# Per-column scale vectors spread over the partitions by TensorE instead of VectorE's stream shuffle

## The chip, the cores and the metric

The kernel runs on one core of a Trainium2 chip. The time is the device time of that core in microseconds (us), the median of several runs. A core has TensorE (PE; matmuls, whose results go to the accumulator memory PSUM), VectorE (DVE), ScalarE (ACT), GpSimd (POOL), SyncE (SP), and DMA engines that move data between HBM and the on-chip memory SBUF. SBUF has 128 partitions. GpSimd, SyncE and ScalarE issue the transfers, each in the order of its own program.

## The reference

Attention with 16 query heads and 4 key heads on 8 batches, and then a residual block with a token mix and a channel mix. All inputs are f32.

```python
x = attention(q, k, v)                     # per batch: 384 tokens x 1024 columns
a1 = alpha1 * x + beta1                    # alpha1, beta1, alpha2, beta2, lam: 1024 columns each
tok = w_tok @ a1                           # 384 x 384 over the tokens
u = x + lam * tok
a2 = alpha2 * u + beta2
ch = relu(a2 @ w_ch1) @ w_ch2              # 1024 -> 4096 -> 1024
out = u + lam * ch
```

The five vectors have one number per column. Where VectorE multiplies a tile that has tokens on the partitions, it needs each vector in every one of the 128 partitions: a `vecs` tile of 128 x 4 x 1024 f32 with g1 = alpha1 * lam, h1 = beta1 * lam, al2 = alpha2 and lam. How that tile is filled is what the change is about.

## The kernel before

W2 stays in SBUF (loaded once, in 16 pieces). W1 is loaded anew for each batch in 16 chunks of 512 KB (in SBUF, bf16), into a ring of 5. The loads turn f32 into bf16 and are issued by GpSimd. Batch 0's attention and token mix are a lead-in; then for each batch a pass over W1 (line 400, `h`) and one over W2 (line 438, `ch`) follow, and the attention of the next batch is woven into the W2 part. In the lead-in, `at[i]` lists what stands after the i-th group of scores in the program. Each `yield` of a pass is a numbered place, at which `turns` hangs work.

```python
vecs = const.tile([P, 4, DM], f32, tag="vecs", name="vecs")
g1, h1, al2, lam_t = (vecs[:, i] for i in range(4))
...
def load_w1(n):                                    # chunk n into the ring, issued by GpSimd
    t = sb.tile([P, NDT, CW * P], bf, tag="w1", name="w1", bufs=RING)
    nc.gpsimd.dma_start(out=t, in_=w1src[:, :, c * CW * P:(c + 1) * CW * P])
...
nc.vector.memset(vecs[:, 0:4:3, :512], 0.0)
def load_vec(i, ap, lo, n):                        # the vector into partitions 0, 32, 64, 96
    nc.sync.dma_start(out=vecs[0:P:32, i, lo:lo + n],
                      in_=bass.AP(tensor=ap.tensor, offset=ap.offset + lo, ap=[[0, 4], [1, n]]))
load_vec(0, moe_alpha1, 0, 512)
load_vec(3, moe_lam, 0, 512)
...
def spread(i, half):                               # from there into the other 31 of each 32
    t = vecs[:, i, half * 512:(half + 1) * 512]
    nc.vector.stream_shuffle(out=t, in_=t, mask=[0] * 32)
def scale(i, half, eng=nc.gpsimd):                 # times lam
    t, m = (vecs[:, j, half * 512:(half + 1) * 512] for j in (i, 3))
    eng.tensor_tensor(out=t, in0=t, in1=m, op=MUL)
...
load_q4(3)                                         # GpSimd's program from here
place_k(0, 0, (0,))
units = side(0)
for f in units[:8]: f()                            # lead-in, first units
scale(0, 0)
load_w1(0)
load_w1(1)
place_k(0, 1)
split()                                            # beta1 * lam as three bf16 rows, for the bias
nc.gpsimd.memset(stage[:, 2120:2824], 0.0)
nc.gpsimd.memset(vecs[:, 0:4:3, 512:], 0.0)
load_vec(0, moe_alpha1, 512, 512)
load_vec(3, moe_lam, 512, 512)
load_w1(2)
load_w1(3)
nc.gpsimd.memset(vecs[:, 1:3], 0.0)
load_w1(4)
load_k(1)
load_vec(1, moe_beta1, 0, DM)
load_vec(2, moe_alpha2, 0, DM)
load_q(1)
load_v(1)
for i in range(3): load_w2(0, i, 8)
for f in units[8:]: f()
...
# in main(0), after chunk c of W1:
if b or c + RING < NCH:
    load_w1(b * NCH + c + RING)                    # into the ring place that chunk c has left
# loading of the third batch's q, in main(1):
if b == 1 and c in range(1, 5):
    load_q(2, [G * (c - 1)])
```

The last lines, and the turning of the third batch's q by TensorE, are in both kernels.

Of the kernel before, what the change touches and what calls it, by code (L numbers as in the profile page):

```python
# [12 lines left out]
def kernel(  # L13
# [21 lines left out]
    nc = tc.nc  # L35
    f32 = mybir.dt.float32
    bf = mybir.dt.bfloat16
    EXP = mybir.ActivationFunctionType.Exp
    RELU = mybir.ActivationFunctionType.Relu
    MUL = mybir.AluOpType.mult  # L40
    ADD = mybir.AluOpType.add
    SUB = mybir.AluOpType.subtract
# [4 lines left out]
    DM = Hq * D  # L47
    DFF = moe_w_ch1.shape[1]
    P = 128
# [4 lines left out]
    NP = Hq // 2  # L54
# [3 lines left out]
    RING = 5  # L58
# [13 lines left out]
    ident = const.tile([P, P], bf, tag="ident", name="ident")  # L72
# [3 lines left out]
    vecs = const.tile([P, 4, DM], f32, tag="vecs", name="vecs")  # L76
# [54 lines left out]
    def load_w1(n):  # L131
        if n < B * NCH:
            t = sb.tile([P, NDT, CW * P], bf, tag="w1", name="w1", bufs=RING)
            c = n % NCH
            nc.gpsimd.dma_start(out=t, in_=w1src[:, :, c * CW * P:(c + 1) * CW * P])  # L135
            w1_tiles[n] = t
# [5 lines left out]
    def bank(shape, tag, name, dtype=f32):  # L142
        if tag == "three":
            return threes[0].tile(shape, dtype, tag="sc", name=name, bufs=3)
        if tag == "mm":
            return mms.tile(shape, dtype, tag="mm", name=name, bufs=2)
        return psum.tile(shape, dtype, tag=tag, name=name, bufs=2 if tag == "sc" else 1)
# [9 lines left out]
    def evac(eng):  # L157
        return nc.scalar.copy if eng == "ACT" else nc.vector.tensor_copy
# [16 lines left out]
    def side(b):  # L175
# [136 lines left out]
        def rows_r(tag):  # L312
            ps = bank([P, 512], tag, "r")
            for st in range(NST):
                nc.tensor.matmul(out=ps[:32, :S], lhsT=ones, rhs=wtokT[:, st, :], start=(st == 0),
                                 stop=(st == NST - 1))
            turned = ps[:, S:S + 2 * NP].rearrange("p (i n) -> p i n", i=2)
            for i, c in enumerate((2, 3)):
                nc.tensor.matmul(out=turned[:, i], lhsT=rows_f[:NP, c * P:(c + 1) * P], rhs=ident_f[:NP, :NP],
                                 is_transpose=True, start=True, stop=True, skip_group_check=True)  # L320
            t = hTf[:32, 7296:7296 + S]
            nc.scalar.copy(out=t, in_=ps[:32, :S])
            nc.vector.scalar_tensor_tensor(out=R[:32], in0=t, scalar=masks[2], in1=ps[:32, :S], op0=MUL, op1=ADD)
            nc.vector.tensor_copy(out=al2T, in_=turned[:, 0])
            nc.vector.tensor_copy(out=a2T[:, :, S:S + 1], in_=turned[:, 1, :, None])

        us = []

        def add(f, *a):
            us.append(lambda: f(*a))  # L330
# [11 lines left out]
        if not first:  # L342


            turns = {24 + 8 * i: [(q_transpose, 2 * i, 2, "three")] for i in range(4)} if b == 2 else {}
            if b == 1:
                turns = {4: [(spread, 1, 0)], 6: [(spread, 1, 1)], 8: [(scale, 1, 0), (scale, 1, 1), (spread, 2, 0)],
                         10: [(spread, 2, 1)], 12: [(k_transpose, 0)], 16: [(q_transpose, 0, 2, "av")],
                         20: [(k_transpose, 2)]}
                for i in range(3):  # L350
                    turns[24 + 4 * i] = [(q_transpose, 2 + 2 * i, 2, "av")]
            return turns, {
                0: [(scores3, 0)], 4: [(av, 0)], 6: [(scores3, 1)], 8: [(tok_flip, 0)], 11: [(av, 1)],
                13: [(scores3, 2, True)], 15: [(av, 2)], 16: [(tok_flip, 1)], 18: [(tok_flip, 2)], 19: [(av, 3)],
                21: [(scores3, 3)], 23: [(tok_flip, 3)], 25: [(av, 4)], 27: [(scores3, 4)], 29: [(tok_flip, 4)],
                31: [(av, 5)], 33: [(scores3, 5, True)], 35: [(av, 6), (tok_flip, 5)], 37: [(av, 7)],
                39: [(tok_flip, 6)], 41: [(tok_flip, 7)]}
        add(k_transpose, 0, 1)
        add(q_transpose, 0, 1, "av", "ACT")
        add(place_k, 0, 0, (1,))  # L360
        add(q_transpose, 1, 1, "tp")
        ut = a2_transpose
        at = {0: [(warmup, 3), (spread, 0, 0), (spread, 3, 0)], 1: [(k_transpose, 1, 1)],
              2: [(q_transpose, 2, 2, "av")], 3: [(warmup, 1)],
              4: [(av, 0)], 5: [(a1, 0)], 6: [(av, 1), (k_transpose, 2, 2, "tp")],
              7: [(q_transpose, 4, 2, "av"), (a1, 1)], 8: [(av, 2)],
              9: [(wtok_transpose, 0, "av"), (wtok_transpose, 1, "tp")],
              10: [(wtok_transpose, 2, "av"), (q_transpose, 6, 2, "mm"), (fill_h, 0)], 11: [(av, 3), (rows_r, "tp")],
              12: [(a1, 2)], 13: [(tok, 0), (av, 4), (a1, 3)],
              14: [(tok, 1), (spread, 0, 1), (spread, 3, 1), (scale, 0, 1, nc.vector), (ut, 0)], 15: [(a1, 4), (av, 5), (tok, 2), (a1, 5), (fill_h, 4)], 16: [(ut, 1), (tok, 3)],  # L370
              17: [(ut, 2), (av, 6), (a1, 6)]}
        for i in range(18):
            add(scores, i)
# [76 lines left out]
    with tc.manual_schedule(engines=order):  # L450
# [9 lines left out]
        load_k(0, [0])  # L460

        hTf = hT.rearrange("p n s -> p (n s)")
        rows_f = hTf[:32, 9216:10240].bitcast(f32)
        rows_t = hTf[:32, 10240:10496].bitcast(f32)
        rows_b = hTf[:32, 10496:10624]
        stage = sb.tile([P, NST * DM], f32, tag="x", name="stage", bufs=2)
        qst = stage[:, :G * NST * D].rearrange("p (h st d) -> p h st d", h=G, st=NST)
        wtok_in = stage[:, 1536:2112].bitcast(bf).rearrange("p (tt s) -> p tt s", tt=NST)
# [4 lines left out]
        ones = stage[:, 2824:2840].bitcast(bf)  # L473
        masks = [stage[:32, 2840 + i:2841 + i] for i in range(3)]
        sel4 = stage[:32, 2844:2848].bitcast(bf)
        nc.vector.memset(vecs[:, 0:4:3, :512], 0.0)

        def load_row(i, ap, n=4):
            nc.sync.dma_start(out=rows_f[:n * NP, i * P:(i + 1) * P],
                              in_=bass.AP(tensor=ap.tensor, offset=ap.offset, ap=[[0, n], [P, NP], [1, P]]))  # L480


        def load_vec(i, ap, lo, n):
            nc.sync.dma_start(out=vecs[0:P:32, i, lo:lo + n],
                              in_=bass.AP(tensor=ap.tensor, offset=ap.offset + lo, ap=[[0, 4], [1, n]]))

        load_vec(0, moe_alpha1, 0, 512)
        load_vec(3, moe_lam, 0, 512)
        load_k(0, [2])
        load_row(0, moe_lam)  # L490
        load_row(1, moe_beta1)
        load_row(2, moe_alpha2, 1)
        load_row(3, moe_beta2, 1)
        for h in (0, 2):
            nc.scalar.dma_start(out=qst[:, h:h + 2], in_=q[0, h:h + 2].rearrange("h (p st) d -> p h st d", st=NST))
        xs[0] = sb.tile([P, NST, DM], f32, tag="x", name="x", bufs=2)
# [10 lines left out]
        AX = mybir.AxisListType.X  # L507
# [2 lines left out]
            nc.vector.tensor_reduce(out=m, in_=ident[:32, 8 * (i + 1):24 + 8 * (i // 2)], op=ADD, axis=AX)  # L510
        nc.vector.tensor_scalar(out=masks[2], in0=masks[2], scalar1=-1.0, scalar2=None, op0=MUL)
        with nc.allow_low_precision("ones and zeros"):
            nc.vector.tensor_reduce(out=sel4, in_=ident[:32, :32].rearrange("p (k c) -> p c k", c=NP), op=ADD, axis=AX)


        def spread(i, half):
            t = vecs[:, i, half * 512:(half + 1) * 512]
            nc.vector.stream_shuffle(out=t, in_=t, mask=[0] * 32)  # L518

        def scale(i, half, eng=nc.gpsimd):  # L520
            t, m = (vecs[:, j, half * 512:(half + 1) * 512] for j in (i, 3))
            eng.tensor_tensor(out=t, in0=t, in1=m, op=MUL)


        def split():
            r = rows_f[:, P:2 * P]
            nc.gpsimd.tensor_tensor(out=r, in0=r, in1=rows_f[:, :P], op=MUL)
            for src, dst, m in ((r, rows_t, masks[0]), (rows_t, r, masks[1])):
                nc.gpsimd.tensor_copy(out=rows_b, in_=src)
                nc.gpsimd.tensor_scalar(out=dst, in0=rows_b, scalar1=m, scalar2=None, op0=MUL)  # L530
                nc.gpsimd.tensor_tensor(out=dst, in0=dst, in1=src, op=SUB)
            nc.gpsimd.tensor_copy(out=rows_b, in_=r)


        def fill_h(p):
            nc.vector.tensor_tensor(out=H[:32, p * P:(p + 4) * P].rearrange("p (n d) -> p n d", n=4),
                                    in0=rows_b[:, None, :].to_broadcast([32, 4, P]),
                                    in1=sel4[:, p:p + 4, None].to_broadcast([32, 4, P]), op=MUL)

        load_v(0)  # L540
# [1 line left out]
        nc.gpsimd.dma_start(out=wtok_in, in_=moe_w_tok.rearrange("(p tt) s -> p tt s", tt=NST))  # L542
        load_q4(3)
        place_k(0, 0, (0,))
        units = side(0)
        for f in units[:8]:
            f()
        scale(0, 0)
        load_w1(0)
        load_w1(1)  # L550
        place_k(0, 1)
        split()
        nc.gpsimd.memset(stage[:, 2120:2824], 0.0)
        nc.gpsimd.memset(vecs[:, 0:4:3, 512:], 0.0)
        load_vec(0, moe_alpha1, 512, 512)
        load_vec(3, moe_lam, 512, 512)
        load_w1(2)
        load_w1(3)
        nc.gpsimd.memset(vecs[:, 1:3], 0.0)  # L559
        load_w1(4)  # L560
        load_k(1)
        load_vec(1, moe_beta1, 0, DM)
        load_vec(2, moe_alpha2, 0, DM)
        load_q(1)
        load_v(1)
        for i in range(3):
            load_w2(0, i, 8)
        for f in units[8:]:
            f()
        place_k(1, 0)  # L570
        place_k(1, 1)
# [45 lines left out]
```

The softmax here doesn't subtract the row's maximum and nothing guards it: scores larger than these inputs give would overflow.

## Time and profile before

| what | value |
|---|---|
| median of 3 runs | 808.59 us (808.38 to 808.82) |
| span of the profiled run | 807.0 us |
| W1 matmuls, line 400 | x2016, 35% of the chain that ended last |
| W2 matmuls, line 438 | x1600, 41% of it |
| stream shuffles, line 518 | x8, median 725 ns each, between 6.9 and 44 us |
| products with lam, line 522 | x3 on GpSimd, median 1272 ns; x1 on VectorE, 692 ns |
| memsets of `vecs` on GpSimd, lines 554 and 559 | 941 and 1845 ns |

An engine's name with "q" is its queue of issued transfers, PEld is the load of a matmul's weights. In a list of waits, a line names the engine and source line that waited, what it waited for, the total, how often, and the longest. The chain of waits follows the work that ended last back to its causes: an engine in it did work that the end depended on. Idle time of an engine outside the chain costs nothing by itself. The granted TensorE clock was 1.00 in every stretch.

### The profile page before, as it was taken

Reading aid. Unit: us, or ns where it says so; the run is one execution under the profiler, and the core shown is the slowest. Engines: PE = TensorE matmul, PEld = TensorE weight load, DVE = VectorE, ACT = ScalarE, POOL = GpSimd, SP = SyncE. Lnnn points to the kernel's source line nnn. Section 1 sums busy time; section 2 is a strip of 40 time slices with the busy share of each in tenths; the row PEclk is TensorE's granted clock in tenths of the full one; section 3 lists DMA queues with packets and bytes.
Section 4 is the critical chain, followed back from the end, with each engine's and each line's share of the span. In section 5 each row is a group of like instructions: output and inputs, shape, how many; then the busy total and the mean of one; then the engine's idle time right before and its main releaser. Section 6 shows DMA issues by size and latency. Waiting matters only on the chain.

```text
span 807.0 us, 14228 instructions
## 1 busy us (share of the span) xinstructions
PE 794.0 (98%) x6123; PEld 452.2 (56%) x6123; DVE 344.9 (43%) x669; ACT 223.0 (28%) x302; POOL 189.9 (24%) x247
## 2 busy tenths in 40 slices
PE   8989999999999999999999999999999999999998
PEld 4755555555556555565555655556555655556545
DVE  7753465224652265422663236622366224652122
ACT  7522431224312324123321233222331224312100
POOL 8534220433003410135002350023400330003000
DMA  9999997999159982899529992399914995129611
GB/s 149 195 205 201 211 205 129 194 195 168 56 124 185 198 118 61 144 186 197 81 71 170 187 196 59 86 170 197 171 42 110 166 196 94 48 58 185 86 40 40
DMA packets 231767, 112.42 MB, mean 139 GB/s; under 512 B 81200, under 2 KB 225536, under 8 KB 231704
## 3 DMA queue, kind: packets, MB, share of 16 engines
q0 software_dynamic: 170752, 83.47, 78.4%
q1 hardware_dynamic: 60408, 27.65, 13.5%
q8 instruction: 48, 0.79, 0.4%
q10 hardware_dynamic: 544, 0.39, 0.2%
q14 instruction: 15, 0.12, 0.0%
HBM read 170.57 MB, written 12.58 MB: 227 GB/s over the span
## 4 chain that ended last, share of the span: by engine, by line
PE 88%; DMA 8%; POOL 2%; issue 1%; DVE 0%; POOLq 0%
PE ch L438 41%; PE h L400 35%; DMA w<-in_moe_w_ch_dram 6%; PE sc L218 4%; PE sc L253 4%; PE sc L276 3%; DMA q_raw<-in_q_dram 1%; POOL w L135 1%; PE warm L455 0%; PE tp L204 0%; POOL w L140 0%; POOL vecs L559 0%; POOL q_raw L117 0%; DVE vecs L518 0%; POOL hT L530 0%
## 5 line engine op out<-in xcount | busy, mean ns | idle before, releaser
L438 PE MATMUL ch<-w,hT 128*128 128x512 bf16 (+2 forms) x1600 | 357.6, 371 | 1.4 <-DVE o L443 0.9
L400 PE MATMUL h<-a2T,w 128*128 128x384 bf16 (+1 forms) x2016 | 331.8, 326 | 4.4 <-DMA w<-in_moe_w_ch_dram 4.2
L400 PEld LDWEIGHTS <-w 128*128 128x128 bf16 x2016 | 196.4, 98 | 135.9 <-DMA w<-in_moe_w_ch_dram 6.2
L135 POOL DMA_DIRECT2D w<-in_moe_w_ch_dram x128 | 112.3, 878 | 537.2 <-PE h L400 519.1
L438 PEld LDWEIGHTS <-hT 128*128 128x128 bf16 x1600 | 144.8, 98 | 153.1 <-issue 10.5
L227 ACT ACTIVATE es<-sc 128x1024 bf16<-128x1024 f32 x126 | 121.4, 1023 | 188.2 <-PE sc L218 179.4
L410 DVE TENSOR_SCALAR hT<-h,bias 128x384 bf16<-128x384 f32 x128 | 79.1, 618 | 215.4 <-PE h L400 214.8
L408 ACT ACTIVATE hT<-h,bias 128x384 bf16<-128x384 f32 x128 | 74.4, 581 | 306.7 <-PE h L400 306.2
L443 DVE TENSOR_TENSOR o<-ch,vecs 128x512 f32<-128x512 f32 (+2 forms) x50 | 33.5, 669 | 109.4 <-PE ch L438 109.4
L253 PEld LDWEIGHTS <-es 128*128 128x128 bf16 x1008 | 38.2, 97 | 13.2
L276 PEld LDWEIGHTS <-wtokT 128*128 128x128 bf16 x576 | 37.2, 98 | 13.6 <-DVE a L266 1.7
L218 PE MATMUL sc<-qT,kT 64*128 64x384 bf16 (+2 forms) x576 | 41.9, 272 | 0.8 <-ACT hT L227 0.7
L253 PE MATMUL sc<-v,es 128*128 128x65 bf16 x1008 | 39.8, 193 | 0.0
L258 DVE RECIPROCAL rinv<-sc 128x6 f32<-128x6 f32 x56 | 10.8, 193 | 67.2 <-PE sc L253 66.3
L283 DVE TENSOR_TENSOR x<-sc,x 128x384 f32<-128x384 f32 x56 | 30.9, 552 | 19.9 <-PE sc L276 19.9
L276 PE MATMUL sc<-a,wtokT 128*128 128x128 bf16 x504 | 37.3, 219 | 0.0
L218 PEld LDWEIGHTS <-kT 64*128 64x128 bf16 x576 | 21.7, 94 | 24.6 <-issue 19.3
L444 DVE TENSOR_TENSOR o<-o,x 128x512 f32<-128x512 f32 (+2 forms) x50 | 33.5, 670 | 1.7
L287 DVE TENSOR_TENSOR a<-x,vecs 128x384 bf16<-128x384 f32 x56 | 31.5, 562 | 1.9
L266 DVE TENSOR_TENSOR a<-a1f,vecs 128x384 bf16<-128x384 f32 x56 | 31.4, 561 | 2.1
L264 DVE TENSOR_TENSOR a1f<-x,vecs 128x384 f32<-128x384 f32 x56 | 31.2, 558 | 1.9
L259 DVE TENSOR_TENSOR x<-sc,rinv 128x384 f32<-128x384 f32 x56 | 31.2, 557 | 1.9
(78 smaller groups left out, 213.1 us busy)
## 6 DMA issues: line engine op xcount, KB each, us to landing
w<-in_moe_w_ch_dram POOLq DMA_DIRECT2D x144, 512.0 KB, 8.7
out_dram<-o SPq DMA_DIRECT2D x47, 256.0 KB, 2.2
q_raw<-in_q_dram POOLq DMA_DIRECT2D x28, 192.0 KB, 8.3
kst<-in_k_dram SPq DMA_DIRECT2D x16, 192.0 KB, 3.0
v<-in_v_dram POOLq DMA_DIRECT2D x24, 64.0 KB, 8.0
a2T<-a SPq DMA_TRANSPOSE x56, 2.3
qg<-in_q_dram POOLq DMA_DIRECT2D x3, 192.0 KB, 4.5
stage<-in_q_dram ACTq DMA_DIRECT2D x2, 192.0 KB
```

The lines of the kernel that those rows point to most:

```text
L135: nc.gpsimd.dma_start(out=t, in_=w1src[:, :, c * CW * P:(c + 1) * CW * P])
L218: nc.tensor.matmul(out=sc[:, hh, k % 4:k % 4 + n], lhsT=kT[r, sk, 2 * p // G, :], rhs=qT[r, p, st:st + n, :], start=True, stop=True)
L227: nc.scalar.activation(out=e, in_=sc, func=EXP, scale=scale_qk)
L253: nc.tensor.matmul(out=av[:, hh, sq, :], lhsT=ess[k // 4][:, m % 2, k % 4, :], rhs=vb[:, sk, hk, :], start=(sk == 0), stop=(sk == NST - 1))
L276: nc.tensor.matmul(out=ps[:, tt, :], lhsT=wtokT[:, st, tt * P:(tt + 1) * P], rhs=a1s[p][:, st, :], start=(st == 0), stop=(st == NST - 1 an ...
L287: nc.vector.tensor_tensor(out=a2s[p], in0=u, in1=bc(al2, p), op=MUL)
L400: nc.tensor.matmul(out=ps[:, :n], lhsT=w1[:, dt, j * P:(j + 1) * P], rhs=a2T[:, dt, :n], start=(dt == 0), stop=(dt == NDT - 1))
L408: nc.scalar.activation(out=hT[:, nt, :], in_=ps[:, :S], func=RELU, bias=c1)
L410: nc.vector.tensor_scalar(out=hT[:, nt, :], in0=ps[:, :S], scalar1=c1, scalar2=0.0, op0=ADD, op1=mybir.AluOpType.max)
L438: nc.tensor.matmul(out=ps[:, lo:hi], lhsT=hT[:, nt, ms * P:(ms + 1) * P], rhs=w2[:, nt, dw * 512 + lo:dw * 512 + hi], start=(nt == 0), sto ...
L443: nc.vector.tensor_tensor(out=o[:, lo:hi], in0=ps[:, lo:hi], in1=lam_t[:, c], op=MUL)
L444: nc.vector.tensor_tensor(out=o[:, lo:hi], in0=o[:, lo:hi], in1=x[:, ms, c], op=ADD)
```

## The change

The vectors are no longer shuffled. Each is loaded as rows: row p holds columns 128p to 128p + 127, so a vector is 8 partitions x 128, and most are loaded four times over into 32 partitions. Rows are scaled by lam and split by VectorE (or GpSimd) into three bf16 parts whose sum is the f32 value; the parts lie in rows p, p + 8 and p + 16. A matmul with a column of ones at these three rows, repeated 128 times as its weights (`sel`), sums the parts and writes the row into all 128 partitions of PSUM, from where it is copied to `vecs`. It is meant to take the shuffles, their memsets and the products over 128 partitions off VectorE and GpSimd. In the first pass the matmuls for h1, al2 and lam hang at places 34 to 54, with ScalarE's copies.

```diff
-        nc.vector.memset(vecs[:, 0:4:3, :512], 0.0)
-        load_vec(0, moe_alpha1, 0, 512)
-        load_vec(3, moe_lam, 0, 512)
+        sel = stage[:, 2852:2856].bitcast(bf)
+        for t in (stage[:, 2120:2824], rows_b, sel):
+            nc.vector.memset(t, 0.0)
+        load_row(0, moe_alpha1)
+        load_row(3, moe_lam)
         load_k(0, [2])
-        load_row(0, moe_lam)
         load_row(1, moe_beta1)
-        load_row(2, moe_alpha2, 1)
-        load_row(3, moe_beta2, 1)
+        load_row(2, moe_alpha2)
+        load_row(4, moe_beta2, 1)
 ...
+        def spread(ps_, vs, tag, eng="DVE"):
+            n = len(ps_)
+            ps = bank([P, 4, P], tag, "vec")
+            w = vs[1] - vs[0]
+            for i, p in enumerate(ps_):
+                nc.tensor.matmul(out=ps[:, i * w:(i + 1) * w], lhsT=sel[:, p:p + 1].to_broadcast([P, P]),
+                                 rhs=rows_b[:, vs[0] * P:vs[1] * P], start=True, stop=True)
+            evac(eng)(out=vecs[:, vs[0]:vs[1], ps_[0] * P:(ps_[-1] + 1) * P].rearrange("p v (n d) -> p n v d", n=n),
+                      in_=ps[:, :n * w].rearrange("p (n v) d -> p n v d", n=n))
 ...
-                turns = {4: [(spread, 1, 0)], 6: [(spread, 1, 1)], 8: [(scale, 1, 0), (scale, 1, 1), (spread, 2, 0)],
-                         10: [(spread, 2, 1)], 12: [(k_transpose, 0)], ...
+                turns = {4: [(split, 2, 4, 0)], 8: [(split, 2, 4, 1)], 12: [(k_transpose, 0)], ...
+                for i in range(4):
+                    turns[34 + 4 * i] = [(spread, (2 * i, 2 * i + 1), (1, 3), "tp", "ACT")]
+                for i in range(2):
+                    turns[50 + 4 * i] = [(spread, range(4 * i, 4 * i + 4), (3, 4), "av", "ACT")]
 ...
-        at = {0: [(warmup, 3), (spread, 0, 0), (spread, 3, 0)], 1: [(k_transpose, 1, 1)],
-              2: [(q_transpose, 2, 2, "av")], 3: [(warmup, 1)],
+        at = {0: [(warmup, 3), (scale_rows, 0), (split, 0, 1, 0)], 1: [(k_transpose, 1, 1), (split, 0, 1, 1)],
+              2: [(q_transpose, 2, 2, "av")], 3: [(warmup, 1), (spread, lower, (0, 1), "tp")],
 ...
-              12: [(a1, 2)], 13: [(tok, 0), (av, 4), (a1, 3)],
-              14: [(tok, 1), (spread, 0, 1), (spread, 3, 1), (scale, 0, 1, nc.vector), (ut, 0)], 15: [(a1, 4), (av, 5), ...
+              12: [(spread, upper, (0, 1), "av"), (a1, 2)], 13: [(tok, 0), (av, 4), (a1, 3)],
+              14: [(tok, 1), (ut, 0), (a1, 4)], 15: [(av, 5), (tok, 2), ...
 ...
+        def split(lo, hi, step=None, eng=nc.vector):
+            c = slice(lo * P, hi * P)
+            for i, m in enumerate(masks[:2]):
+                if step in (None, i):
+                    src, dst = (rows_t, rows_f) if i else (rows_f, rows_t)
+                    eng.tensor_copy(out=rows_b[:32, c], in_=src[:, c])
+                    ...   # dst = rows_b * m - src; on GpSimd as a product and a subtraction
+            if step != 0:
+                eng.tensor_copy(out=rows_b[:32, c], in_=rows_f[:, c])
 ...
-        units = side(0)
-        for f in units[:8]:
-            f()
-        scale(0, 0)
         load_w1(0)
         load_w1(1)
         place_k(0, 1)
-        split()
-        nc.gpsimd.memset(stage[:, 2120:2824], 0.0)
-        nc.gpsimd.memset(vecs[:, 0:4:3, 512:], 0.0)
-        load_vec(0, moe_alpha1, 512, 512)
-        load_vec(3, moe_lam, 512, 512)
-        load_w1(2)
-        load_w1(3)
-        nc.gpsimd.memset(vecs[:, 1:3], 0.0)
-        load_w1(4)
+        scale_rows(1, nc.gpsimd)
+        split(1, 2, None, nc.gpsimd)
+        for c in range(2, RING):
+            load_w1(c)
         load_k(1)
-        load_vec(1, moe_beta1, 0, DM)
-        load_vec(2, moe_alpha2, 0, DM)
         load_q(1)
         load_v(1)
```

More of the change, by code (lines that the diff above doesn't have):

```diff
@@ L317, in rows_r @@
             turned = ps[:, S:S + 2 * NP].rearrange("p (i n) -> p i n", i=2)
-            for i, c in enumerate((2, 3)):
+            for i, c in enumerate((2, 4)):
                 nc.tensor.matmul(out=turned[:, i], lhsT=rows_f[:NP, c * P:(c + 1) * P], rhs=ident_f[:NP, :NP],
@@ L346, in side @@
             if b == 1:
-                turns = {4: [(spread, 1, 0)], 6: [(spread, 1, 1)], 8: [(scale, 1, 0), (scale, 1, 1), (spread, 2, 0)],
-                         10: [(spread, 2, 1)], 12: [(k_transpose, 0)], 16: [(q_transpose, 0, 2, "av")],
-                         20: [(k_transpose, 2)]}
+                turns = {4: [(split, 2, 4, 0)], 8: [(split, 2, 4, 1)], 12: [(k_transpose, 0)],
+                         16: [(q_transpose, 0, 2, "av")], 20: [(k_transpose, 2)]}
                 for i in range(3):
                     turns[24 + 4 * i] = [(q_transpose, 2 + 2 * i, 2, "av")]
+                for i in range(4):
+                    turns[34 + 4 * i] = [(spread, (2 * i, 2 * i + 1), (1, 3), "tp", "ACT")]
+                for i in range(2):
+                    turns[50 + 4 * i] = [(spread, range(4 * i, 4 * i + 4), (3, 4), "av", "ACT")]
             return turns, {
@@ L361, in side @@
         add(q_transpose, 1, 1, "tp")
+        lower, upper = range(NP // 2), range(NP // 2, NP)
         ut = a2_transpose
-        at = {0: [(warmup, 3), (spread, 0, 0), (spread, 3, 0)], 1: [(k_transpose, 1, 1)],
-              2: [(q_transpose, 2, 2, "av")], 3: [(warmup, 1)],
+        at = {0: [(warmup, 3), (scale_rows, 0), (split, 0, 1, 0)], 1: [(k_transpose, 1, 1), (split, 0, 1, 1)],
+              2: [(q_transpose, 2, 2, "av")], 3: [(warmup, 1), (spread, lower, (0, 1), "tp")],
               4: [(av, 0)], 5: [(a1, 0)], 6: [(av, 1), (k_transpose, 2, 2, "tp")],
@@ L368, in side @@
               10: [(wtok_transpose, 2, "av"), (q_transpose, 6, 2, "mm"), (fill_h, 0)], 11: [(av, 3), (rows_r, "tp")],
-              12: [(a1, 2)], 13: [(tok, 0), (av, 4), (a1, 3)],
-              14: [(tok, 1), (spread, 0, 1), (spread, 3, 1), (scale, 0, 1, nc.vector), (ut, 0)], 15: [(a1, 4), (av, 5), (tok, 2), (a1, 5), (fill_h, 4)], 16: [(ut, 1), (tok, 3)],
+              12: [(spread, upper, (0, 1), "av"), (a1, 2)], 13: [(tok, 0), (av, 4), (a1, 3)],
+              14: [(tok, 1), (ut, 0), (a1, 4)], 15: [(av, 5), (tok, 2), (a1, 5), (fill_h, 4)], 16: [(ut, 1), (tok, 3)],
               17: [(ut, 2), (av, 6), (a1, 6)]}
@@ L462 @@
         hTf = hT.rearrange("p n s -> p (n s)")
-        rows_f = hTf[:32, 9216:10240].bitcast(f32)
-        rows_t = hTf[:32, 10240:10496].bitcast(f32)
-        rows_b = hTf[:32, 10496:10624]
+        rows_f = hTf[:32, 9216:10496].bitcast(f32)
+        rows_t = hTf[:32, 10496:11520].bitcast(f32)
+        rows_b = hTf[:, 11520:12032]
         stage = sb.tile([P, NST * DM], f32, tag="x", name="stage", bufs=2)
@@ L480, in load_row @@
                               in_=bass.AP(tensor=ap.tensor, offset=ap.offset, ap=[[0, n], [P, NP], [1, P]]))
-        def load_vec(i, ap, lo, n):
-            nc.sync.dma_start(out=vecs[0:P:32, i, lo:lo + n],
-                              in_=bass.AP(tensor=ap.tensor, offset=ap.offset + lo, ap=[[0, 4], [1, n]]))
-        load_vec(0, moe_alpha1, 0, 512)
-        load_vec(3, moe_lam, 0, 512)
+        load_row(0, moe_alpha1)
+        load_row(3, moe_lam)
         load_k(0, [2])
-        load_row(0, moe_lam)
         load_row(1, moe_beta1)
-        load_row(2, moe_alpha2, 1)
-        load_row(3, moe_beta2, 1)
+        load_row(2, moe_alpha2)
+        load_row(4, moe_beta2, 1)
         for h in (0, 2):
@@ L512 @@
         with nc.allow_low_precision("ones and zeros"):
[L513 to L522, printed above, removed]
@@ L525, in split @@
[L525 to L532, printed above, removed]
+            for t, n in ((sel, 24), (sel4, 32)):
+                nc.vector.tensor_reduce(out=t[:n], in_=ident[:n, :n].rearrange("p (k c) -> p c k", c=NP), op=ADD, axis=AX)
@@ new lines, in scale_rows @@
+        def scale_rows(i, eng=nc.vector):
+            r = rows_f[:, i * P:(i + 1) * P]
+            eng.tensor_tensor(out=r, in0=r, in1=rows_f[:, 3 * P:4 * P], op=MUL)
+        def split(lo, hi, step=None, eng=nc.vector):
[4 more added lines that the diff above has]
+                    eng.tensor_copy(out=rows_b[:32, c], in_=src[:, c])
+                    if eng is nc.vector:
+                        eng.scalar_tensor_tensor(out=dst[:, c], in0=rows_b[:32, c], scalar=m, in1=src[:, c],
+                                                 op0=MUL, op1=SUB)
+                    else:
+                        eng.tensor_scalar(out=dst[:, c], in0=rows_b[:32, c], scalar1=m, scalar2=None, op0=MUL)
+                        eng.tensor_tensor(out=dst[:, c], in0=dst[:, c], in1=src[:, c], op=SUB)
+            if step != 0:
+                eng.tensor_copy(out=rows_b[:32, c], in_=rows_f[:, c])
@@ L535, in fill_h @@
         def fill_h(p):
             nc.vector.tensor_tensor(out=H[:32, p * P:(p + 4) * P].rearrange("p (n d) -> p n d", n=4),
-                                    in0=rows_b[:, None, :].to_broadcast([32, 4, P]),
+                                    in0=rows_b[:32, None, P:2 * P].to_broadcast([32, 4, P]),
                                     in1=sel4[:, p:p + 4, None].to_broadcast([32, 4, P]), op=MUL)
@@ L567 @@
             load_w2(0, i, 8)
-        for f in units[8:]:
+        for f in side(0):
             f()
```

## The prediction

> **What bounds the kernel now.** I read the page first, then TensorE's waits, then the chain of waits in order of time, then the stretches of 2 us in the first 50 us. The page says where the time is:
>
> ```profile
> span 807.0 us, 14228 instructions
> PE 794.0 (98%) x6123; PEld 452.2 (56%) x6123; DVE 344.9 (43%) x669; ACT 223.0 (28%) x302; POOL 189.9 (24%) x247
> ```
>
> TensorE is busy for 794.0 of 807.0 us, and the two big matmul lines (W2 and W1) hold 41% and 35% of the chain. A busy TensorE is not TensorE at its peak, but the change touches none of these matmuls: seven of the eight batches keep their instructions. So what can be won lies in TensorE's idle time, 13 us in all, and only in the part of it that the first batch causes. The list of what TensorE waited for names that part:
>
> ```profile
> PE h L400 <- DMA w<-in_moe_w_ch_dram: 4.2, 4, 2.3
> ...
> PE tok L276 <- DVE x L259: 1.2, 1, 1.2
> ...
> PE ch L438 <- DMA w<-in_moe_w_ch_dram: 0.5, 1, 0.5
> ```
>
> (total, number, longest, in us). The timeline places them: 2.26 us at 49.43 for W1 chunk 5; 0.40, 0.55 and 0.95 us at 157 to 165 for W1 chunks of the second batch; 0.47 us at 88.72 for a piece of W2; 1.23 us at 26.18 for VectorE. The chain of waits says why chunk 5 is late:
>
> ```profile
> 17.44 0.89 POOL vecs L554
> 18.33 1.82 POOL w L135 x2
> 20.15 1.82 POOL vecs L559
> 21.96 0.81 POOL w L135
> 22.77 1.44 POOL q_raw L117 x2
> 24.21 11.14 DMA q_raw<-in_q_dram
> ...
> 38.64 10.75 DMA w<-in_moe_w_ch_dram
> ```
>
> (start, us, what). GpSimd issues nearly all loads, and two memsets of the scale vectors stand between the W1 loads. The same moments in the table of stretches (columns: stretch, length, busy PE, PEld, DVE, ACT, POOL, PE clock, DMA share, GB/s):
>
> ```profile
> 16.00:18.00 2.00, 1.90 (x35) 1.46 (x34) 1.75 (x5) 2.00 (x3) 1.92 (x4) 1.00 1.07 141
> 18.00:20.00 2.00, 1.53 (x19) 0.81 (x17) 1.70 (x7) 1.67 (x4) 2.00 (x3) 1.00 0.04 8
> 20.00:22.00 2.00, 2.00 (x43) 1.74 (x42) 1.73 (x5) 1.44 (x3) 2.00 (x3) 1.00 1.07 121
> 22.00:24.00 2.00, 2.00 (x40) 1.59 (x37) 2.00 (x6) 1.98 (x3) 2.00 (x3) 1.00 1.34 220
> ```
>
> The reader is to see a hole: GpSimd is full, and the transfers fall to 8 GB/s. After 22 us they run at about 200 GB/s without a break until about 112 us. Everything behind the hole is late by its size. Against 200 GB/s the hole lacks (59 + 192 + 79) GB/s over 2 us each, which is 0.66 MB, or 3.3 us.
>
> VectorE's own delay is in the timeline:
>
> ```profile
> 22.75 0.72 DVE L518 STREAM_SHUFFLE vecs<-vecs 128x512 f32<-128x512 f32 x1
> 23.39 0.72 DVE L518 STREAM_SHUFFLE vecs<-vecs 128x512 f32<-128x512 f32 x1
> 24.14 0.69 DVE L522 TENSOR_TENSOR vecs<-vecs 128x512 f32<-128x512 f32 x1
> 24.87 0.56 DVE L270 TENSOR_TENSOR hT<-x,vecs 128x384 bf16<-128x384 f32 x1
> 25.34 0.19 DVE L258 RECIPROCAL rinv<-av 128x6 f32<-128x6 f32 x1
> 25.57 0.56 DVE L259 TENSOR_TENSOR x<-av,rinv 128x384 f32<-128x384 f32 x1
> ```
>
> Two shuffles and a product stand for 2.1 us before the multiply that frees the accumulator; TensorE restarts at 26.18.
>
> **What the Trainium skill says.** "DMA: Bandwidth & Descriptors", section "Anatomy of one DMA", says that DMA engines do not wait on semaphores: a wait happens on the issuing sequencer before dispatch. That is the hole: the data path was free, the issuer was not; the trace agrees (8 GB/s while GpSimd was busy 2.00 of 2.00 us). "VectorE: DVE Perf Modes", section "The perf-mode tier table", gives the stream shuffle one speed only, about 2400 ns for 2048 columns. A quarter of it is 600 ns; the trace has 722 to 740 ns for 512 columns. "GPSIMD Engine Reference", section 4.1, puts a two-input operation on GpSimd at about twice VectorE's time; the trace has 1271 ns against 692 ns for the same 128x512 product. "TensorE: Matmul & The Clock Gate", section "Back-to-back issue gap", measures about 81 ns for a weight load and a 128-column matmul. The trace shows less: the six transposes before 50.43 us took 0.33 us, 55 ns each. I use 55 ns.
>
> **The change part by part.**
>
> *GpSimd, removed.* Before the first W1 load: one product of 1.27 us and the wait of 1.16 us for the shuffles; so W1 chunks 0 and 1 are issued at about 7.2 instead of 9.58. Before chunk 2: also the memsets of 0.67 and 0.94 us. The 4.5 us of split arithmetic on the beta1 row stay. It then ends about 2.4 us earlier, at 14.4, and chunk 2 follows at once: 14.4 instead of 18.28, 3.9 us. Chunk 4 no longer waits for the 1.84 us memset: 5.7 us. The second batch's q follows it, about 17 instead of 22.73. In the main pass two products (2.51 us at 42.98) go, ahead of the issue at 45.43. The hole is thus filled and the saturated stream behind it starts 3.3 us earlier.
>
> *VectorE in the lead-in.* Removed: four shuffles (about 2.75 us in place), one product (0.69) and a memset of 1024 columns (0.91). Added: memsets of 704, 256 and 4 columns (about the same 0.9), six operations on 32x128 (a product, three casts, two multiply-subtracts; at 0.2 us each 1.2 us, an estimate from 0.23 for a 128x128 cast and 0.56 for a 384-column operation) and two evacuations of 128x512 at about 0.7. The first half trades 1.37 us of shuffles for 1.2 us in two parts, so it is even. In the second half 2.1 us before the multiply at 25.57 become one 0.7 us evacuation at about 19.8. That is 1.4 us less ahead of the stalled multiply, so the wait of 1.23 goes. But the evacuation delays the accumulators around 21 us by up to 0.35. Net 0.9 us.
>
> *TensorE, added.* Eight 128-column matmuls in the lead-in: four where ScalarE's exponentials set the pace (twelve without a gap from 6.97 to 18.28), four just after. In the first pass eight of 256 columns and eight of 128: 8 x 0.108 + 8 x 0.055 = 1.3 us (0.108 is half of a 512-column matmul's 0.216 in the chain). TensorE is dense there, so these 1.3 us count in full. The six ScalarE copies, about 0.7 us each, lie in the middle of odd column blocks, with ScalarE's only work there the previous block's 0.16 + 0.58: hidden.
>
> *The waits.* Chunk 5 is issued when the lead-in ends, about 37.7 instead of 38.64. It would land 3.3 us earlier, at about 46.1. TensorE needs it at 47.2 - 0.9 = 46.3. So the wait of 2.26 is gone, with little to spare: I count 2.2. At 88.7 the W2 piece is 3.3 us earlier, TensorE about 0.9 + 2.2 - 1.3 = 1.8 us, so the 0.47 goes too: 0.4. The second batch's 1.9 us stay: between 112 and 136 us the W1 ring is full and the lead in transfers is lost.
>
> Sum: 0.9 + 2.2 + 0.4 - 1.3 = 2.2 us. 808.6 - 2.2 = 806.4 us.
>
> **The rivals.**
>
> *The wait only moves.* For chunk 5 the margin is 0.2 us. If GpSimd's queue holds no more transfers than now (it already waits for landings at 29.88 and 32.55 in the lead-in), the lead shrinks and 1 to 2 us of the wait come back, or appear at chunk 6. Then 807.5 to 808.5. Against it: those waits are in a saturated stretch, so they move with the stream.
>
> *TensorE becomes the bound of the spread.* The lower-half spread stands in TensorE's program before the first scores that feed the exponentials. If the six small operations end after about 10.0 us, ScalarE runs dry. Six at 0.3 rather than 0.2 us would cost about 0.5 us. And if each of the 24 matmuls costs 0.1 us more for a turn of the array, 2.4 us more: 808 to 809. For it: every group interrupts a stream of another shape. Against it: the transposes interrupt the same stream now, for 0.33 us per six.
>
> *More is won than counted.* If TensorE's waits for chunks in the second batch also shrink, up to 1.9 us more: 804.5. Against it: 155 GB/s at 112 to 136 us, against 187 in the 45 us that follow, shows a queue that has caught up.
>
> **The range and the chances.** Two of the three gains (chunk 5, VectorE) are read straight from waits; the loss is exact to about 0.5 us. The sum could lose 1 to 2 us to the first two rivals and win 1.5 to the third. So 806.4, with 804.7 to 808.7 for 8 times in 10. A step of 2% is 16.2 us, more than TensorE's whole idle time: faster 0.01, same 0.98, slower 0.01.
>
> **What would show it.** Right: no stretch between 12 and 24 us under about 120 GB/s; chunk 2 issued near 14.4 and the second batch's q near 17; no wait for W1 at 47 to 49; no VectorE wait at 25; the 24 added matmuls at 2 us in sum or less; the second batch's waits still near 1.9. The prediction is wrong if the wait for chunk 5 is still over 1 us, if the exponentials show gaps before 18 us, or if TensorE waits in the lead-in for the split rows.

## The result and the profile after

The kernel after takes 805.73 us (median of 4 runs, 805.0 to 806.5) against 808.71 us before: a ratio of 0.9961, 95% interval 0.9943 to 0.9978. Two more measurements of the same kernel on other occasions gave 0.9959 (0.9947 to 0.9972) and 0.9964 (0.9952 to 0.9977). By the medians that is 3.0, 3.7 and 2.9 us. It is a small gain, and all three intervals lie below 1.

The page of the kernel after:

```profile
span 804.7 us, 14264 instructions
PE 795.0 (99%) x6147; PEld 454.0 (56%) x6147; DVE 345.3 (43%) x668; ACT 226.6 (28%) x308; POOL 182.1 (23%) x241
```

TensorE has 24 matmuls more and is busy 1.0 us longer, in a span that is 2.3 us shorter. Its waits (what waited, for what; total, number, longest, in us):

```profile
PE h L415 <- DMA w<-in_moe_w_ch_dram: 2.3, 3, 1.0
PE warm L470 <- DVE wtokT L473: 1.5, 1, 1.5
PE vec L333 <- DVE hT L546: 1.1, 1, 1.1
PE ch L453 <- DVE o L458: 0.9, 2, 0.5
```

The wait of 2.26 us for W1 chunk 5, that of 0.47 us for the W2 piece and that of 1.23 us for VectorE are gone. The three waits for W1 that are left are all in the second batch. A new one stands in the list: the spread matmuls wait 1.1 us for the split rows. The table of stretches (stretch, length, busy PE, PEld, DVE, ACT, POOL, PE clock, DMA share, GB/s):

```profile
16.00:18.00 2.00, 1.95 (x37) 1.35 (x35) 1.84 (x6) 2.00 (x4) 2.00 (x3) 1.00 1.46 199
18.00:20.00 2.00, 2.00 (x26) 1.02 (x23) 1.51 (x4) 1.72 (x3) 2.00 (x4) 1.00 1.46 199
20.00:22.00 2.00, 1.87 (x38) 1.51 (x37) 1.98 (x7) 1.52 (x3) 0.56 (x2) 1.00 1.46 197
22.00:24.00 2.00, 2.00 (x39) 1.62 (x39) 1.96 (x4) 1.79 (x3) 0.53 (x1) 1.00 1.48 205
```

The hole is closed: 199, 199 and 197 GB/s where there were 141, 8 and 121. And the end of the lead-in in the chain of waits (start, us, what):

```profile
36.37 0.65 PE h L169 x4
37.04 0.81 PE h L169 x4
37.85 5.88 PE h L415 x36
```

No transfer stands in the chain here, where before 10.75 us of W1 loading did. How far TensorE is ahead of the kernel before, by the start of the same work in both timelines:

| mark on TensorE | before, us | after, us | ahead, us |
|---|---|---|---|
| first W1 matmul behind the lead-in | 38.50 | 37.69 | 0.81 |
| first turning of q in the pass (behind chunk 5) | 50.10 | 46.52 | 3.58 |
| first W2 matmul | 79.86 | 77.61 | 2.25 |
| first W1 matmul of the second batch | 135.44 | 132.65 | 2.79 |
| first W2 matmul of the second batch | 181.05 | 178.45 | 2.60 |

From row to row one reads the gains and losses: 0.81 from the lead-in, 2.77 with the wait for chunk 5, 1.33 lost to the spread matmuls, 0.54 from W2, 0.19 lost in the second batch. At the last mark 2.60 us are left, somewhat less than the difference of the medians; where the rest lies is not traced.

### The profile page after: what moved, and what is told of

Its sections match the earlier page's. It is cut to its first block, busy times and chain, and to the rows that moved or that the text cites. A ratio compares the mean times of both kernels' runs of the same rounds, so it can differ in the third digit from the quotient of the medians.

```text
span 804.7 us, 14264 instructions
## 1 busy us (share of the span) xinstructions
PE 795.0 (99%) x6147; PEld 454.0 (56%) x6147; DVE 345.3 (43%) x668; ACT 226.6 (28%) x308; POOL 182.1 (23%) x241
## 4 chain that ended last, share of the span: by engine, by line
PE 96%; DMA 2%; DVE 1%; issue 0%; ACT 0%; POOL 0%; POOLq 0%
PE ch L453 42%; PE h L415 39%; PE sc L218 4%; PE sc L253 4%; PE sc L276 3%; DMA w<-in_moe_w_ch_dram 2%; PE h L169 1%; PE tp L204 0%; PE tok L276 0%; PE av L253 0%; PE warm L470 0%; PE ut L293 0%; PE vec L333 0%; DVE hT L540 0%; PE tok L280 0%
## 5 line engine op out<-in xcount | busy, mean ns | idle before, releaser
L458 DVE TENSOR_TENSOR o<-ch,vecs 128x512 f32<-128x512 f32 (+2 forms) x50 | 33.5, 669 | 108.0 <-PE ch L453 108.0
L459 DVE TENSOR_TENSOR o<-o,x 128x512 f32<-128x512 f32 (+2 forms) x50 | 33.5, 670 | 1.7
```

The costliest lines, as they stand in the source:

```text
L458: nc.vector.tensor_tensor(out=o[:, lo:hi], in0=ps[:, lo:hi], in1=lam_t[:, c], op=MUL)
L459: nc.vector.tensor_tensor(out=o[:, lo:hi], in0=o[:, lo:hi], in1=x[:, ms, c], op=ADD)
```

## The experiments

The main theory: the gain comes from where GpSimd's work on the scale vectors stood, ahead of the loads that it issues. The main rival: it comes from taking the shuffles off VectorE, which held up TensorE at 25 us.

**GpSimd's work put back (`e1_memsets_back`).** The kernel after with memsets of scale vectors that are not yet in use.

```diff
+        nc.gpsimd.memset(vecs[:, 1:3], 0.0)
+        nc.gpsimd.memset(vecs[:, 1, :512], 0.0)
         load_w1(0)
 ...
-        for c in range(2, RING):
-            load_w1(c)
+        nc.gpsimd.memset(vecs[:, 1:3], 0.0)
+        load_w1(2)
+        load_w1(3)
+        nc.gpsimd.memset(vecs[:, 1:3], 0.0)
+        load_w1(4)
```

> The kernel after, with GpSimd memsets of the still unused scale vectors put back at the places where GpSimd worked in the kernel before: about 2.7 us ahead of W1 chunk 0 and 1.84 us each ahead of chunks 2 and 4. The result is unchanged, VectorE and TensorE keep the new way. Theory (the late loads are what the change repaired): a hole in the transfers near 18 to 22 us again, W1 chunk 5 makes TensorE wait about 2.3 us, 0.4 us more at the W2 piece; time up by 2 to 2.9 us against the kernel after, that is at or just above the kernel before. Rival (VectorE's shuffles out of the lead-in are what it repaired): within 0.6 us of the kernel after.

Measured: 808.88 us, 1.0004 of the kernel before (0.9996 to 1.0012). Four memsets, 6.0 us of GpSimd time, took back the whole gain, although VectorE and TensorE kept the new way. W1 chunk 2 was issued at 18.36 us and the second batch's q at 22.81, as in the kernel before (18.28 and 22.73). The hole in the transfers is there again, and so is the wait (the stretch, the list of waits, the timeline):

```profile
18.00:20.00 2.00, 2.00 (x26) 1.21 (x25) 1.54 (x5) 1.62 (x4) 2.00 (x3) 1.00 0.56 81
...
PE h L415 <- DMA w<-in_moe_w_ch_dram: 4.8, 4, 2.5
...
47.89 0.83 PE L415 MATMUL h<-a2T,w 128*128 128x385 bf16 x4 [2.50 <-DMA w<-in_moe_w_ch_dram]
```

The last line is chunk 5. The lead-in ended at 37.05 us, earlier than in the kernel after: the shorter lead-in was worth nothing, as the next chunk was not there.

**Part of GpSimd's order changed in the kernel before (`e2_before_loads_first`).**

```diff
+        load_w1(2)
         nc.gpsimd.memset(vecs[:, 0:4:3, 512:], 0.0)
         load_vec(0, moe_alpha1, 512, 512)
         load_vec(3, moe_lam, 512, 512)
-        load_w1(2)
         load_w1(3)
-        nc.gpsimd.memset(vecs[:, 1:3], 0.0)
         load_w1(4)
 ...
+        nc.gpsimd.memset(vecs[:, 1:3], 0.0)     # and its two loads, behind the first W2 issues
```

> The kernel before with its shuffles, only GpSimd's order changed: W1 chunk 2 ahead of the 0.94 us memset, chunks 3 and 4, the second batch's k, q and v and the first W2 pieces ahead of the 1.84 us memset, whose vectors are loaded after it. Chunk 4 and q come 1.8 us earlier. Theory of the late loads: the hole shrinks by about half, the wait for chunk 5 falls from 2.26 to about 0.7, time down 1.2 to 1.8 us against the kernel before. Rival (the shuffles): no change, since they all stay.

Measured: 810.6 us, 1.0015 (1.0007 to 1.0023): a miss. Its VectorE timeline shows the first part of the loss:

```profile
23.79 0.01 DVE L518 LOAD_MASK_SELECT vecs<-vecs  x1 [0.85 <-DMA vecs<-in_moe_alpha_dram]
...
24.90 0.01 DVE L518 LOAD_MASK_SELECT vecs<-vecs  x1 [0.36 <-DMA vecs<-in_moe_lam_dram]
```

The memset ahead of the vectors' own small loads came 1.1 us later (18.47 against 17.39), so the upper halves of alpha1 and lam landed late, behind W1. VectorE stood still before both shuffles, and TensorE waited 2.63 us for it instead of 1.23. It went on at 27.70 us, 1.52 later than in the kernel before. The larger part of the lead-in's delay is the granted clock behind that wait (the third number from the right is the clock):

```profile
26.00:28.00 2.00, 0.30 (x4) 0.31 (x5) 1.93 (x5) 0.18 (x1) 0.00 (x0) 0.70 1.27 220
28.00:30.00 2.00, 2.00 (x17) 1.39 (x16) 1.72 (x4) 0.20 (x1) 0.00 (x0) 0.50 1.44 205
30.00:32.00 2.00, 2.00 (x28) 1.94 (x27) 0.41 (x2) 1.30 (x2) 0.74 (x1) 0.50 1.56 190
32.00:34.00 2.00, 2.00 (x15) 1.63 (x14) 1.38 (x3) 0.52 (x1) 0.64 (x1) 0.60 1.60 190
```

The same matmuls took longer there (three of line 276 0.50 us instead of 0.34), and the lead-in ended at 42.71 us, 4.21 later than before: the 1.52, and 2.69 in these stretches. Eleven of the fifteen executions had a mean granted clock of 0.998 or less, and the three at 1.000 took 808.7 to 809.8 us, about the time of the kernel before on that occasion (809.05 us). The wait for chunk 5 was gone, but the lead-in had become slower than the load. With small loads, issue order and clock all moved, this run does not separate the theories: the miss speaks neither for the main one nor against it.

**All shuffles kept, GpSimd freed (`e7_shuffle_early_loads`).** The cleaner form of the same question.

```diff
-        nc.vector.memset(vecs[:, 0:4:3, :512], 0.0)
+        nc.vector.memset(vecs[:, 0:4:3], 0.0)
-        load_vec(0, moe_alpha1, 0, 512)              # lam likewise
+        load_vec(0, moe_alpha1, 0, DM)
 ...
-        scale(0, 0)                                  # on GpSimd, ahead of load_w1(0)
+        # at[2]: (scale, 0, 0, nc.vector)
 ...
-        nc.gpsimd.memset(vecs[:, 0:4:3, 512:], 0.0)  # and the loads behind it
         load_w1(2); load_w1(3)
-        nc.gpsimd.memset(vecs[:, 1:3], 0.0)
         load_w1(4)
 ...
+        nc.gpsimd.memset(vecs[:, 1:3], 0.0)          # behind the first W2 issues
```

> The kernel before with all eight shuffles kept, but with GpSimd freed ahead of the loads: VectorE clears the whole of g1 and lam at the start (0.9 us more there), scales the lower half of g1 itself, and the 1.84 us memset stands behind the first W2 issues. W1 chunks 0 and 1 near 7.1, chunks 2 to 4 near 14.5 us. Theory (the place of GpSimd's work ahead of the loads is the whole of it): no hole, no wait for chunk 5 nor at the W2 piece, 2.5 us faster than the kernel before, about 806.2, although no shuffle is gone. Rival (the shuffles have to go, since they hold VectorE and TensorE at 25 us): at most 0.5 us faster than the kernel before.

The kernel after was measured beside it (`after_again`).

> The kernel after once more, beside the three that follow: 805.7 us, and the ratio to the kernel before 0.996, as measured first. It is what the three are compared with.

It gave 805.73 us and 0.9959, and `e7_shuffle_early_loads` 807.11 us, 0.9974 (0.9965 to 0.9983). That is 2.3 us faster than the kernel before with every shuffle in place, of the 3.7 us that the kernel after gained on this occasion. Its waits, the stretch of the hole, and the first matmuls of the pass, of which the 49th is the first of chunk 5:

```profile
PE tok L276 <- DVE x L259: 1.2, 1, 1.2
...
PE av L253 <- DMA v<-in_v_dram: 0.9, 1, 0.9
...
PE ch L438 <- DMA w<-in_moe_w_ch_dram: 0.3, 1, 0.3
...
18.00:20.00 2.00, 1.78 (x22) 0.87 (x18) 1.52 (x4) 1.67 (x3) 2.00 (x4) 1.00 1.38 181
...
38.90 6.37 PE L400 MATMUL h<-a2T,w 128*128 128x385 bf16 x36
45.44 2.78 PE L400 MATMUL h<-a2T,w 128*128 128x385 bf16 x16
```

TensorE's 1.2 us behind the shuffles is there still, and the lead-in ended at 38.90 us, later than before. The gain came with the wait for chunk 5 gone: TensorE ran through. The first W1 issue was at 8.23 us instead of the planned 7.1, since the first batch's v was issued later. So the rival, as put, falls: the shuffles didn't have to go. The theory is right for most of the gain. What the shuffles themselves cost is not separated: the lead-in ended 1.21 us later than in the kernel after, but the wait of 0.9 us for v in it comes from this edit.

**The first pass's spread undone (`e3_pass_by_shuffle`, `e3_again`).**

```diff
-                turns = {4: [(split, 2, 4, 0)], 8: [(split, 2, 4, 1)], ...
-                for i in range(4):
-                    turns[34 + 4 * i] = [(spread, (2 * i, 2 * i + 1), (1, 3), "tp", "ACT")]
-                for i in range(2):
-                    turns[50 + 4 * i] = [(spread, range(4 * i, 4 * i + 4), (3, 4), "av", "ACT")]
+                turns = {4: [(shuffle, 3, 0)], 8: [(shuffle, 3, 1)], ...
+                for i in range(2):
+                    turns[36 + 4 * i] = [(shuffle, 1, i)]
+                    turns[44 + 4 * i] = [(shuffle, 2, i)]
+                    turns[52 + 4 * i] = [(scale, 1, i)]
 ...
+        nc.gpsimd.memset(vecs[:, 1:4], 0.0)     # behind the first W2 issues, then three load_vec
```

> The kernel after with the first pass's sixteen spread matmuls, the six ScalarE copies and the VectorE splits of that pass undone: h1, al2 and lam are loaded into four partitions and spread there by six stream shuffles and two products on VectorE, with their memset on GpSimd behind the first W2 issues. Theory (each spread matmul costs TensorE its stream time in full, 1.3 us in sum): 1.3 us faster than the kernel after. Rival (the spread lies in a stretch that waits for W1 transfers anyway, so its time is hidden): within 0.4 us of the kernel after.

> The first pass's scale vectors by shuffles once more, beside the kernel after. In its first trace W2 began 1.33 us earlier and the second batch's waits took back 0.3, while the medians differed by 0.3 only, from different chips. Theory (TensorE's stream time counts in full, less those 0.3): 1.0 us faster than the kernel after. Rival (hidden): within 0.4 us.

Beside the second measurement stood the kernel after (`after_third`).

> The kernel after beside the two that follow: about 805.7 us.

Measured: 805.43 us at first (0.9955, 0.9942 to 0.9967); then 805.16 us (804.55 to 805.49; 0.9948, 0.9935 to 0.9962) beside the kernel after at 806.49 us (806.29 to 806.67). The pair of the same occasion is 1.33 us apart and does not overlap. In the first trace the lead-in took as long as in the kernel after (first W1 matmul at 37.68), and the first W2 matmul stood here:

```profile
76.28 1.03 PE L453 MATMUL ch<-w,hT 128*128 128x512 bf16 x4
```

That is 1.33 us earlier than 77.61, the stream time of the sixteen matmuls, and the second batch's waits took 0.3 of it back. TensorE's time here is not hidden; 4.3 us of shuffles and 1.4 us of products on VectorE, which has room in this pass, cost less. The clean reading is this first trace. That the medians of the second pair differ by 1.33 us too does not show the same thing: in the trace of `e3_again` the lead-in too ended 1.33 us earlier (36.36), which the edit does not touch, and W2 began 2.16 us earlier. By the medians the gain is 0.3 us (the first time, measured on different occasions) or 1.3; its size stays open between these.

**The split rows behind the turned q (`e4_split_after_q`).**

```diff
-        1: [(k_transpose, 1, 1), (split, 0, 1, 1)],
-        2: [(q_transpose, 2, 2, "av")], 3: [(warmup, 1), (spread, lower, (0, 1), "tp")],
-        4: [(av, 0)],
+        1: [(k_transpose, 1, 1)],
+        2: [(q_transpose, 2, 2, "av"), (split, 0, 1, 1)], 3: [(warmup, 1)],
+        4: [(av, 0), (spread, lower, (0, 1), "tp")],
```

> The kernel after with the second half of the first split behind the copy of the turned q in VectorE's program, and the lower spread behind the first attention-times-v in TensorE's. Theory (the lead-in lost time because the exponentials ran dry behind the split rows, 0.75 us on ScalarE): the gap at 10.5 us goes and the lead-in ends 0.4 to 0.8 us earlier; the time falls by as much. Rival (the lead-in is set by TensorE and VectorE after 18 us, and ScalarE's gap is made up there): the gap goes, but the first W1 matmul behind the lead-in stays within 0.2 us of 37.7, and the time with it.

The kernel after shows what it was aimed at:

```profile
7.35 0.74 DVE L538 CAST hT<-hT 32x128 bf16<-32x128 f32 x1
...
8.84 1.03 POOL L107 CAST k<-kst 128x384 bf16<-128x384 f32 x2
8.99 1.02 DVE L540 SCALAR_TENSOR_TENSOR hT<-hT,stage 32x128 f32<-32x128 bf16 x1
...
10.46 0.40 PE L333 MATMUL vec<-hT,stage 128*128 128x128 bf16 x4 [1.08 <-DVE hT L546]
...
11.25 7.57 ACT L227 ACTIVATE hT<-sc 128x1024 bf16<-128x1024 f32 x8 [0.75 <-PE sc L218]
```

In this execution the exponentials stand still for 0.75 us because the next scores are behind the spread in TensorE's program, and q's copy behind the split in VectorE's. With the edit the twelve exponentials run without a gap, and the lead-in ends at 37.09 us instead of 37.69. From the first exponential (6.91 against 6.72, which differs by when the loads land) it is 0.79 us shorter. The median is 805.70 us (0.9957, 0.9943 to 0.997): the time did not follow by an amount that these runs resolve. Nor is the gap in every execution: in the trace of `e3_again`, whose lead-in has the program of the kernel after, the first exponential began at 6.25 us, the second multiply-subtract of the split was over before GpSimd's casts began (8.52 against 8.85), and all twelve ran without a gap.

**GpSimd's cast of k moved (`e6_k_cast_later`).**

```diff
         load_w1(1)
+        load_w1(2)
         place_k(0, 1)
 ...
-        for c in range(2, RING):
+        for c in range(3, RING):
```

> The kernel after with one edit on GpSimd: W1 chunk 2 is issued ahead of the two casts of k, which then run near 9.8 to 10.8 instead of 8.84 to 9.87 us. Theory (VectorE's split operations were slow because each waits for a GpSimd operation that runs at the time): the multiply-subtract at 8.99 us takes 0.34 instead of 1.02 us, TensorE's wait of 1.08 us for the split rows falls to 0.4, and the lead-in ends 0.3 to 0.7 us earlier. Rival (the operation is slow by itself, or for another cause in VectorE): it stays at about 1.0 us.

Its timeline, VectorE and GpSimd:

```profile
9.00 0.34 DVE L540 SCALAR_TENSOR_TENSOR hT<-hT,stage 32x128 f32<-32x128 bf16 x1
```

```profile
9.73 1.03 POOL L107 CAST k<-kst 128x384 bf16<-128x384 f32 x2
```

The same operation at the same moment takes 0.34 us once GpSimd's cast is elsewhere, and TensorE's wait for the split rows is gone. The lead-in ends 0.26 us earlier, at 37.43. The time, 805.95 us (0.9962, 0.995 to 0.9975), is that of the kernel after.

**Both edits (`e5_both`, `e5_again`) and the shuffles hung later (`e8_shuffles_late`).** `e3` and `e4` together:

> The two edits that showed a gain in the trace, together: the first pass's scale vectors by shuffles on VectorE, and the second half of the first split behind the copy of the turned q. Sum of the two traces: lead-in 0.6 us shorter, first W2 matmul 0.6 + 1.3 us earlier, of which the second batch's waits take back 0.3: 1.6 us faster than the kernel after, about 804.1. If the earlier lead-in only meets the wait for W1 chunk 5 again, 0.6 us of it is lost.

> Both edits once more, beside the kernel after: 0.9 to 1.6 us faster. If the second edit (lead-in) counts, also 0.3 to 0.6 faster than the run with the shuffles alone.

Measured: 804.80 us (804.37 to 805.18; 0.9946, 0.9933 to 0.9958) beside `after_again` at 805.73; then 805.56 us (804.16 to 806.58; 0.9951, 0.9938 to 0.9965) beside `after_third` at 806.49. Both times 0.93 us faster than the kernel after by the medians, the second time with ranges that overlap; not distinguishable from the shuffles alone. The trace of the second, its slowest execution (806.58 us), shows a wait of the edit's own making on VectorE:

```profile
41.26 0.01 DVE L560 LOAD_MASK_SELECT vecs<-vecs  x1 [2.23 <-DMA vecs<-in_moe_lam_dram]
```

lam, loaded behind the W1 stream, was not there for the shuffle at place 4, and the relu behind it in VectorE's program held TensorE for 1.9 us. In the trace of `e3_again` the same wait was 0.69 us, in that of `e5_both` 0.16. The last run hung the shuffles at places 34 to 52 and the products at 56 and 60:

```diff
-                turns = {4: [(shuffle, 3, 0)], 8: [(shuffle, 3, 1)], 12: [(k_transpose, 0)],
+                turns = {12: [(k_transpose, 0)],
 ...
+                    turns[34 + 2 * i] = [(shuffle, 3, i)]
+                    turns[40 + 4 * i] = [(shuffle, 1, i)]
+                    turns[48 + 4 * i] = [(shuffle, 2, i)]
+                    turns[56 + 4 * i] = [(scale, 1, i)]
```

> Both edits, with all shuffles of the first pass hung at places 34 to 60 instead of from place 4 on. In the second run of both edits the first shuffle waited 2.2 us for lam to land behind the W1 stream, and TensorE 1.9 us for VectorE. Theory: that wait is gone for good, W2's first matmul near 75.3 us as in the first run of both edits, 1.2 us or more faster than the kernel after (0.9945 of the kernel before or less), with runs closer together. Rival (the wait only stood in for another of the same size): as the second run of both edits, 0.995.

Measured: 805.00 us (804.60 to 805.21; 0.9953, 0.994 to 0.9967). The pass has places 0 to 59 only, so the product at place 60 never runs: this kernel leaves out the scaling of h1's upper half (one VectorE operation of 0.68 us, in a stretch where VectorE has room). In its trace the wait for VectorE is gone and W2 begins at 75.46 us, so here the wait did not stand in for another. No run with the place mended was made; what it brings beyond the shuffles alone stays open.

## Why the prediction was right, point by point

The predicted 806.4 us lies 0.7 us from the measured 805.73, inside 804.7 to 808.7; the predicted change of 2.2 us compares with 3.0 by the medians.

- *GpSimd, removed, and the hole.* Right in kind and by `e1`. Chunk 2 was issued at 13.89 us (predicted 14.4), the second batch's q at 16.60 (about 17). Its size was too small: the prediction counted only 16 to 22 us and 0.66 MB. Over 8 to 22 us the kernel before moved 135 GB/s and the kernel after 205: 70 GB/s x 14 us = 0.98 MB, or 4.9 us at 200 GB/s. So the margin for chunk 5 was wider than the 0.2 us of the prediction: with the lead-in over at 36.62 us (`e5_both`) there was still no wait for it.
- *The wait for chunk 5.* Predicted 2.2 us, and 2.77 us were gained between the two marks: the 2.26, and about half a microsecond more, part of it the 0.15 us for which TensorE had waited for VectorE's relu behind a shuffle.
- *TensorE, added.* Predicted 1.3 us in the pass, measured 1.33 from mark to mark and 1.33 again when undone in the first trace of `e3`. The sum of 55 ns and 108 ns for each matmul held; ScalarE's copies were hidden, at 0.59 us each rather than 0.7.
- *VectorE in the lead-in.* The net was right (0.9 predicted, 0.81 measured), its terms were not, and that the sum came out was luck. The six small operations were to take 1.2 us. They took 3.2 us (0.44 + 0.74 + 0.34 + 0.30 + 1.02 + 0.36), and the second rival's first half came true: TensorE waited 1.08 us, ScalarE 0.75. So two of the three signs by which the prediction wanted to be called wrong appeared (a gap in the exponentials before 18 us, and TensorE waiting for the split rows). The exponentials were over 0.54 us later than before (18.82 against 18.28), where no loss was predicted. Behind them the kernel after gained 1.35 us, more than predicted, and the two came to 0.81.
- *The W2 piece.* Its wait is gone, as predicted: 0.4 counted, 0.54 between the marks.
- *The second batch's waits.* Predicted to stay at 1.9 us; they were 2.33. The trend was right (an early W1 ring gains nothing there), and about 0.2 us of the lead was lost:

```profile
154.78 0.82 PE L415 MATMUL h<-a2T,w 128*128 128x384 bf16 x4 [0.83 <-DMA w<-in_moe_w_ch_dram]
...
158.44 2.77 PE L415 MATMUL h<-a2T,w 128*128 128x384 bf16 x16 [0.55 <-DMA w<-in_moe_w_ch_dram]
...
162.17 0.82 PE L415 MATMUL h<-a2T,w 128*128 128x384 bf16 x4 [0.95 <-DMA w<-in_moe_w_ch_dram]
```

- *The rivals.* The wait did not move to another chunk of the first pass. More than was counted was not won in the second batch.

## What to carry to other kernels

When one engine issues the loads, look for its own arithmetic between the issues, and for a stretch in which the transfers stop: what can be won is the wait in which that hole ends (2.26 us here), not the busy share of the engine. Work that prepares operands belongs behind the issues, and its own small loads must not end up behind the big stream, or the engine that needs them stops (`e2`, `e5_again`). The matmuls put into a dense stream cost their stream time in full here; the same work on an engine with room was slower in itself and cheaper in the end (`e3`).

## What the runs showed of the hardware

A short VectorE operation can take as long as the GpSimd operation beside it. In `e1_memsets_back` a 32x128 cast took 0.21 us when it began before a GpSimd memset, and 0.92 us when it began during it:

```profile
7.00 0.21 DVE L538 CAST hT<-hT 32x128 bf16<-32x128 f32 x1
7.25 0.34 DVE L540 SCALAR_TENSOR_TENSOR hT<-hT,stage 32x128 f32<-32x128 bf16 x1
...
8.13 0.92 DVE L538 CAST hT<-hT 32x128 bf16<-32x128 f32 x1
...
7.10 1.87 POOL L559 MEMSET vecs<- 128x2048 f32 x1
```

The late cast ended at 9.05 us, 0.08 us behind the memset, but the multiply-subtract at 7.25 ran through during the memset in its usual 0.34 us. In the kernel after the multiply-subtract begun at 8.99 ended at 10.01, behind GpSimd's casts (to 9.87), and took 0.34 us when they were moved (`e6`). "SBUF — State Buffer" in the Trainium skill, section "Who interferes with whom", says that VectorE and GpSimd share a pair of ports under an exclusive lock. By it a VectorE operation in a two-port mode, which a cast can enter, and a GpSimd operation exclude each other, the later waiting for the whole of the other, while a VectorE operation with two inputs in SBUF contends only with a GpSimd operation that reads SBUF, not with one that only writes it. These cases agree with it: the memset only writes, the casts read. Not every slow operation is explained: the cast at 7.35 us in the kernel after took 0.74 us beside GpSimd's issues of W1, and in `e6` one at 7.18 us took 0.21 us beside such issues. A small operation is not cheap by its size alone, then: what GpSimd does at that moment has to be read too.

The granted clock can fall behind a wait of TensorE. In the trace of `e2_before_loads_first` TensorE stood still from 25.07 to 27.70 us; the clock was 1.00 up to 26.5 us, 0.50 from 27.0 to 33.5, and 1.00 again from 34.0. Up to 800 us no other trace has a stretch of 2 us under 1.00, although TensorE waited 2.50 us in that of `e1_memsets_back` and 2.26 us in that of the kernel before. What decides whether the clock falls is not shown.
